# First-layer rows of blocks 3 to 7: turned by TensorE, or by VectorE on the way through DRAM

## The chip, the core and the metric

The kernel runs on one core of a Trainium2 chip. The time is device microseconds (us) of one execution; the profile is of a separate execution of the same program. Engines are named as the profile names them: PE is TensorE (PEld its weight loads), DVE is VectorE, ACT is ScalarE, POOL is GpSimd, and SP is the engine whose queue issues the transfers.

## What is computed

Two layers, each an attention with a learned feature map followed by a dense part, with the same weights in both layers. There are 2048 rows of 640 values in fp32, 32 heads of 20, and 1536 hidden values.

```
x = x + A(layernorm(x)) ; x = x + B(layernorm(x))        # twice

A: q, k, v = x @ wqkv
   phi(y) = [softmax(y w_phi), softmax(-y w_phi)]        # per head, 20 -> 40
   kv = phi(k)^T v ;  z = sum of phi(k)
   o  = phi(q) kv / (phi(q) z + 1e-6) ;  o @ wo
B: mish(x @ w1 + b1) @ w2
layernorm: (x - mean) / sqrt(var + 1e-5), over the 640 values of a row
```

## The kernel before, in words

**Tiles.** The rows are worked on in 8 blocks (numbered 0 to 7) of 256, each of two tiles (t = 0, 1) of 128 rows. A product is made of three: each operand is split into a high part and the remainder (low part), and high x high, high x low and low x high are added in PSUM. So a projection of one tile to 640 columns is 30 matmuls of 128x320 (L344): 5 pieces of the inner dimension, 2 halves of the columns, 3 products.

**Turned rows.** The matmuls need the rows with the 640 values along the partitions. The class `Transposed` (from L265) holds a block's rows in that form, as five pieces of 128 values by 256 rows. Its method `step` makes two pieces at a time (one in the third step): ScalarE's copy makes the high part `xth`, VectorE's subtraction (L286) makes the low part `xtl`. What a step copies comes from one of two places. If the object was given rows, TensorE transposes them (L280, ten transposes of 128x128 per block, against an identity) into a PSUM tile `one`. If it was given columns, these are tiles in SBUF that hold the rows turned already.

**How rows get turned without TensorE.** `spill_turned` (L311) has VectorE transpose each tile in 32x32 pieces, in place (L315), and stores it with four transfers (L317) to a DRAM tensor, in such an order that the tensor holds the block turned. Its pieces are 32 values, 128 bytes. `load_turned` (L319) reads the block back with three transfers (L325) into the tiles it is given. The dense part uses the pair for its own rows (`n1_d`) and for the second layer's first half (`n2_d`).

**The first half of a layer**, `attend_first` (L387), goes through the blocks. A block has six jobs, one per iteration n of the inner loop: keys of both tiles (k0, k1), values (v0, v1), queries (q0, q1), in an order that differs in blocks 0, 1 and 7. A job is a generator. Its first piece is the projection and ScalarE's copy out of PSUM (the `mm` tile; there are two). In the following iterations `advance` takes every pending job one piece further: maximum, minimum and differences (VectorE, for queries partly GpSimd), exponential (ScalarE), sums and reciprocals (VectorE) and the product (GpSimd, L379). A key job ends with 22 matmuls for the key-value product (L416). A query job ends with VectorE's transpose in place (L425) and four stores to `e_d` (L429). The next query job of the same tile t uses the same SBUF buffer `r`, so its copy out of PSUM waits for these stores.

**The next block's rows** are prepared beside the jobs. In the first layer `fetch_normed` (L390) fetches block b + 1 at n = 0 and takes its row statistics (`norm_stats` L246 on VectorE: L250 and L252; `norm_scale` L255 on GpSimd and VectorE). At n = 2 `normed` (L299) has ScalarE normalize both tiles into tiles `xn`, and at n = 3, 4, 5 the three steps with TensorE's transposes follow. In the second layer `fetch_normed` only calls `load_turned` on `n2_d`, into three `xn` tiles, and the steps at n = 3, 4, 5 read these.

**Buffers.** Two for x (`xt`), four for `xn`, two PSUM tiles `mm`, four PSUM tiles `one`.

**What sets the order.** The whole program stands in one block that a planner schedules: it simulates the engines with modelled times and puts on each engine the earliest instruction of the program that can run then, so that a later one may go ahead of one that waits. Transfers and statistics so come much earlier than written: block 7's x, written at block 6, is fetched in block 4. On the chip each engine then runs its list strictly in order. Two things are fixed by hand: all calls of `act` are chained (L110), so ScalarE does them in the order written, and the second half of the layer, `attend_second` (L553), has a written order for PE and SP.

Of the kernel before, what the change touches and what calls it, by code (L numbers as in the profile page):

```python
# [8 lines left out]
F32 = mybir.dt.float32  # L9
# [9 lines left out]
D = 640  # L19
# [5 lines left out]
BT = 2  # L25
BLK = BT * P
NB = S // BLK
# [15 lines left out]
def kernel(  # L43
# [56 lines left out]

    e_d = [dram.tile([EW, BLK], F32, name=f"e_d{b}") for b in range(NB)]

    n1_d = [dram.tile([D, BLK], F32, name=f"n1_d{b}") for b in range(NB)]
    n2_d = [dram.tile([D, BLK], F32, name=f"n2_d{b}") for b in range(NB)]
    x1_d = dram.tile([S, D], F32, name="x1_d")
# [149 lines left out]
    def norm_scale(b, mvs):  # L255

        ve = work.tile([P, BT], F32, tag="ve", name="ve", bufs=2)
        for t in range(BT):
            nc.gpsimd.tensor_scalar(ve[:, t:t + 1], mvs[t][:, 1:2], LN_EPS, 1.0, op0=ALU.add, op1=ALU.mult)
        nc.gpsimd.tensor_tensor(stats[:, b, 0], ve, neg_half, op=ALU.pow)  # L260
        for t in range(BT):
            nc.vector.scalar_tensor_tensor(stats[:, b, 1, t:t + 1], mvs[t][:, 0:1], -1.0,
                                           stats[:, b, 0, t:t + 1], op0=ALU.mult, op1=ALU.mult)
# [35 lines left out]
    def normed(b, xt):  # L299

        xn = [row_tile() for _ in range(BT)]
        for t in range(BT):
            act(xn[t], xt[:, t, :], AF.Identity,
                                 bias=stats[:, b, 1, t:t + 1], scale=stats[:, b, 0, t:t + 1])
        return Transposed(xn)

    def normalize(b, dst, src):
        for t in range(BT):
            act(dst[t], src[t], AF.Identity, bias=stats[:, b, 1, t:t + 1], scale=stats[:, b, 0, t:t + 1])
# [9 lines left out]
    def load_turned(src, tiles):  # L319

        cols = []
        for c, make in zip(range(0, KD, 2), tiles):
            n = min(2, KD - c)
            cols.append(make()[:, :n * BLK].rearrange("p (k s) -> p k s", k=n))
            nc.sync.dma_start(cols[-1], src[c * P:(c + n) * P].rearrange("(k p) s -> p k s", p=P))  # L325
        return Transposed(cols=cols)
# [55 lines left out]
    def fetch(x_src, b, xt=None):  # L382
        xt = x_tile() if xt is None else xt
        nc.sync.dma_start(xt, row_block(x_src, b))
        return xt

    def attend_first(layer, x_src, first):  # L387


        def fetch_normed(b):  # L390
            if layer:
                return load_turned(n2_d[b], [row_tile] * 3)
            xt = fetch(x_src, b)
            norm_scale(b, [norm_stats(t, xt) for t in range(BT)])
            return xt

        pending = []

        def advance():
            for g in pending[::-1]:  # L400
                try:
                    next(g)
                except StopIteration:
                    pending.remove(g)

        def keys(xts, i, v):
            e = big_tile()
            yield from features(project(xts, i % BT, kv_ws, 0), e, False)
            yield
            if i % BT == 0 and BT < i < NT - BT:  # L410
                yield
            for g in range(G):
                p, n = divmod(g, 2)
                w, m = (120, 64) if g < 10 else (80, 42)
                acc, c = (kva, 120 * p) if p < 4 else (kvz, 120 * (p - 4))
                nc.tensor.matmul(acc[64 * n:64 * n + m, c:c + w], v[:, GW * g:GW * g + m],  # L416
                                 e[:, 120 * g:120 * g + w],
                                 start=(i == 0 and p in (0, 4)), stop=(i == NT - 1),
                                 skip_group_check=True)

        def queries(xts, i, ps=None):
            e = query_tile(i)
            yield from features(project(xts, i % BT, q_ws, 0) if ps is None else ps, e, True)

            nc.vector.transpose(e, e)  # L425
            b, t = divmod(i, BT)
            dst = e_d[b].rearrange("(j f) (t q s) -> t q f j s", f=32, t=BT, s=32)
            for q in range(4):
                nc.sync.dma_start(dst[t, q], e[32 * q:32 * q + 32].rearrange("f (j s) -> f j s", s=32))  # L429
                if b == NB - 1:  # L430
                    yield

        def values(xts, i, v):
            vv = v.rearrange("p (h d) -> p h d", d=DH + 1)
            act(vv[:, :, DH], ident[:, :H], AF.Copy, scale=0.0, bias=1.0)
            if i < BT:
                pv = project(xts, i, kv_ws, D, [one_tile(), one_tile()])
                for c in range(2):
                    act(vv[:, c * H // 2:(c + 1) * H // 2, :DH],
                        pv[c][:, :HC].rearrange("p (h d) -> p h d", d=DH), AF.Copy)  # L440
            else:
                pv = project(xts, i % BT, kv_ws, D)
                act(vv[:, :, :DH].rearrange("p (c h) d -> p c h d", c=2),
                    both(pv).rearrange("p c (h d) -> p c h d", d=DH), AF.Copy)
            yield

        if first is None:
            with tc.manual_schedule(engines={mybir.EngineType.SP}):
                bd = big_tile()[:120, :720].rearrange("p (t c) -> p t c", t=6)
                nc.sync.dma_start(bd[:, :3], phi_bd[:, :3])  # L450
                raw = load_raw(0, range(3))
                xt = fetch_normed(0)
                nc.sync.dma_start(bd[:, 3:], phi_bd[:, 3:])
                raw += load_raw(0, range(3, 6))
                nxt = normed(0, xt).all()
                q_ws = [r2_pair(k) for k in range(KD)]
                fold_phi(q_ws, bd, raw)
                kv_ws = load_v_weights()
                raw = load_raw(1)
            nc.sync.dma_start(mask, head_mask)  # L460
        else:
            nxt, kv_ws = first
            q_ws = load_q_weights()
        for b in range(NB):
            xts = nxt
            order = ("k0", "k1", "v0", "v1", "q0", "q1")
            if b == 0:
                order = ("v0", "q0", "v1", "k0", "q1", "k1")
            elif b == 1:
                order = ("k0", "q0", "k1", "v0", "q1", "v1")  # L470
            elif b == NB - 1:
                order = ("k0", "k1", "v0", "v1", "q0")
            vs = [v_tile() for _ in range(BT)]
            for n, (kind, t) in enumerate(order):
                t = int(t)
                i = b * BT + t
                if b == 0 and n == 1:
                    if layer:
                        load_k_weights(kv_ws)
                if b == 0 and n == 3:  # L480
                    if layer == 0:
                        fold_phi(kv_ws, bd, raw)
                    kva, kvz = one_tile(), one_tile()
                if b == NB - 1 and n == 3:
                    loaded = {0: load(0)}
                if b + 1 < NB:
                    if n == 0:
                        xt = fetch_normed(b + 1)
                    elif n == 2:
                        nxt = xt if layer else normed(b + 1, xt)  # L490
                    elif n > 2:
                        nxt.step()
                g = {"k": lambda: keys(xts, i, vs[t]), "q": lambda: queries(xts, i),
                     "v": lambda: values(xts, i, vs[t])}[kind]()
                next(g)
                advance()
                pending.append(g)
            if b == 1:
                if layer == 0:
                    spill_qk_weights(kv_ws, q_ws)  # L500
                o_ws = load_o_weights()

        def rest():

            ps = [one_tile(), one_tile()]
            project_half(ps[0], xts, 1, q_ws, 0, 0)
            advance()
            advance()
            yield
            project_half(ps[1], xts, 1, q_ws, 0, 1, range(3))  # L510
            yield
            project_half(ps[1], xts, 1, q_ws, 0, 1, range(3, KD))
            pending.append(queries(xts, NT - 1, ps))
            next(pending[-1])
            while pending:
                yield
                advance()

        return kva, kvz, o_ws, loaded, rest()
# [379 lines left out]
```

## Time and profile before

| | |
|---|---|
| median of 3 runs | 1398.45 us (1397.73 to 1398.7) |
| profiled execution | 1396.09 us, of which the span of its instructions is 1394.3 us |
| granted TensorE clock | 0.999 of full speed |
| first layer, first half | from the start to about 271 us |
| second layer, first half | from about 743 to 948 us |
| idle time of ScalarE that ended with a transpose (L280) | 99.6 us, 21 times, over the whole program |

The profile's page gives each engine's busy time over the span. A timeline lists the instructions of a stretch by start, duration, engine, line, and tiles written and read; a note in brackets at the end is idle time of the engine just before, and what ended it. The chain of waits follows the work that ended last back from the end of the program. A matmul's duration there is the time that it is in flight, and the next one starts before it has ended; how far apart they start is what they cost.

### The profile page before, as it was taken

Reading aid. Unit: us, or ns where it says so; the run is one execution under the profiler, and the core shown is the slowest. Engines: PE = TensorE matmul, PEld = TensorE weight load, DVE = VectorE, ACT = ScalarE, POOL = GpSimd, SP = SyncE. Lnnn points to the kernel's source line nnn. Section 1 sums busy time; section 2 is a strip of 40 time slices with the busy share of each in tenths; the row PEclk is TensorE's granted clock in tenths of the full one; section 3 lists DMA queues with packets and bytes.
Section 4 is the critical chain, followed back from the end, with each engine's and each line's share of the span. In section 5 each row is a group of like instructions: output and inputs, shape, how many; then the busy total and the mean of one; then the engine's idle time right before and its main releaser. Section 6 shows DMA issues by size and latency. Waiting matters only on the chain. (4 is left out here: it accounts for less than half of the span.)

```text
span 1394.3 us, 28137 instructions
## 1 busy us (share of the span) xinstructions
PE 1380.7 (99%) x11528; PEld 1367.0 (98%) x11528; DVE 1075.5 (77%) x1820; ACT 583.3 (42%) x973; POOL 440.0 (32%) x334
## 2 busy tenths in 40 slices
PE   7999999999999999999999999999999999999998
PEld 7999999999999999999999999999999999999998
DVE  5797877796698877788769988888767876777775
ACT  4444433321355454545454333332235444444443
POOL 1353443343422221222234434343342211211112
PEclk9999999999999999999999999999999999999999
DMA  8533333689633432343474333357976212333200
GB/s 328 162 79 54 67 52 58 184 228 307 235 86 95 114 84 62 83 114 95 122 261 87 71 57 58 65 107 231 288 257 200 76 25 72 95 95 95 75 22 20
DMA packets 350035, 169.57 MB, mean 122 GB/s; under 512 B 286866, under 2 KB 323458, under 8 KB 349906
## 3 DMA queue, kind: packets, MB, share of 16 engines
q1 hardware_dynamic: 349906, 167.78, 44.2%
q8 instruction: 90, 1.47, 0.4%
q14 instruction: 39, 0.32, 0.1%
HBM read 104.82 MB, written 62.91 MB: 120 GB/s over the span
## 5 line engine op out<-in xcount | busy, mean ns | idle before, releaser
L737 PE MATMUL mm<-r2h,ol 128*128 128x320 f32 x1280 | 304.7, 309 | 0.0
L721 POOL TENSOR_TENSOR ol<-big,ol 128x512 fp32r<-128x512 f32 (+1 forms) x98 | 129.8, 1324 | 483.5 <-ACT ol L720 407.3
L695 PE MATMUL one<-xtl,r1h 128*128 128x256 f32 x960 | 268.2, 279 | 0.0
L695 PE MATMUL one<-xth,r1l 128*128 128x256 f32 x960 | 268.0, 279 | 0.0
L695 PE MATMUL one<-xth,r1h 128*128 128x256 f32 x960 | 265.9, 279 | 0.0
L737 PEld LDWEIGHTS mm<-r2h,ol 128*128 128x128 f32 x1280 | 219.1, 188 | 0.0
L737 PE MATMUL mm<-r2l,ol 128*128 128x320 f32 x640 | 197.3, 309 | 0.0
L344 PE MATMUL mm<-r1h,xth 128*128 128x320 f32 x600 | 187.3, 312 | 0.0
L344 PE MATMUL mm<-r1h,xtl 128*128 128x320 f32 x600 | 186.0, 310 | 0.7 <-DVE xtl L286 0.7
L344 PE MATMUL mm<-r1l,xth 128*128 128x320 f32 x600 | 186.0, 310 | 0.0
L695 PEld LDWEIGHTS one<-xtl,r1h 128*128 128x128 f32 x960 | 180.4, 188 | 0.0
L695 PEld LDWEIGHTS one<-xth,r1l 128*128 128x128 f32 x960 | 180.4, 188 | 0.0
L695 PEld LDWEIGHTS one<-xth,r1h 128*128 128x128 f32 x960 | 179.6, 188 | 0.0
L710 DVE TENSOR_SCALAR big<-big 128x512 f32<-128x512 f32 (+1 forms) x98 | 57.1, 583 | 109.9 <-ACT big L708 109.7
L379 POOL TENSOR_TENSOR r<-r,r 128x1280 f32<-128x1280 f32 x32 | 75.8, 2368 | 163.1 <-DVE r L378 157.3
L737 PEld LDWEIGHTS mm<-r2l,ol 128*128 128x128 f32 x640 | 120.2, 188 | 0.0
L712 ACT ACTIVATE big<-big,two 128x512 f32<-128x512 f32 (+1 forms) x98 | 70.1, 715 | 116.2 <-DVE big L711 116.1
L708 ACT ACTIVATE big<-one,b1s 128x256 f32<-128x256 f32 x192 | 80.8, 467 | 90.1 <-PE one L695 89.6
L720 ACT ACTIVATE ol<-big 128x512 fp32r<-128x512 f32 (+1 forms) x98 | 61.0, 622 | 136.0 <-DVE big L719 135.9
L344 PEld LDWEIGHTS mm<-r1h,xth 128*128 128x128 f32 x600 | 112.8, 188 | 1.3
L344 PEld LDWEIGHTS mm<-r1h,xtl 128*128 128x128 f32 x600 | 112.7, 188 | 1.3 <-DVE xtl L286 1.0
L344 PEld LDWEIGHTS mm<-r1l,xth 128*128 128x128 f32 x600 | 112.8, 188 | 0.1
(129 smaller groups left out, 3156.1 us busy)
## 6 DMA issues: line engine op xcount, KB each, us to landing
e_d<-r SPq DMA_DIRECT2D x128, 160.0 KB, 4.0
big<-e_d SPq DMA_DIRECT2D x32, 640.0 KB, 6.6
x_d<-xt SPq DMA_DIRECT2D x23, 640.0 KB, 3.9
xt<-x_d SPq DMA_DIRECT2D x22, 640.0 KB, 4.3
n_d<-xn SPq DMA_DIRECT2D x176, 80.0 KB, 2.1
xt<-in_x SPq DMA_DIRECT2D x16, 640.0 KB, 5.9
xn<-x_d SPq DMA_DIRECT2D x28, 320.0 KB, 4.2
v<-n_d SPq DMA_DIRECT2D x30, 256.0 KB, 3.3
```

Of the source, the lines that this page charges most:

```text
L344: nc.tensor.matmul(ps[:, :HC], a[:, sl], r, start=(k == 0 and n == 0), stop=(k == KD - 1 and n == 2))
L379: nc.gpsimd.tensor_tensor(eg, eg, r.unsqueeze(2).to_broadcast([P, 2 * H, DH]), op=ALU.mult)
L695: nc.tensor.matmul(ph[:, j, :], l, r, start=(n == 0), stop=(n == 3 * KD - 1))
L708: exps[0] = nc.scalar.activation(part(ta, 0)[:, j - js.start], ph[:, j, :], AF.Exp, bias=b1s[:, 2 * pr + j:2 * pr + j + 1]).ins
L710: nc.vector.tensor_scalar_min(e, e, E_CAP)
L712: nc.scalar.activation(r, n, AF.Ln, bias=two)
L720: nc.scalar.activation(ah[:, js], n, AF.Copy)
L721: nc.gpsimd.tensor_tensor(al[:, js], n, ah[:, js].bitcast(F32), op=ALU.subtract)
L737: nc.tensor.matmul(pys[t][:, c, :HC], l[:, j, sl], r, start=(f == 0 and n == 0), stop=(f == KF - 1 and n == 2))
```

## The change

In the first layer, blocks 3 to 7 take the way through DRAM that the second layer's blocks take. A DRAM tensor `n0_d` is added for each block. A generator `turn(b)` prepares such a block in four pieces: fetch x; statistics and scale; normalize in place, in the x tile; transpose by VectorE, in place, and store to `n0_d`. Block b's loop starts `turn(b + 3)` at n = 4 (the fetch), and the following block's loop runs its other pieces at n = 1, 2 and 3. One block later `fetch_normed` loads the turned rows at n = 0, and the steps at n = 3, 4 and 5 read them from SBUF. Blocks 1 and 2 stay as they were, block 0 too. x still has two buffers.

```diff
@@
+    n0_d = [dram.tile([D, BLK], F32, name=f"n0_d{b}") for b in range(NB)]
     n1_d = [dram.tile([D, BLK], F32, name=f"n1_d{b}") for b in range(NB)]
@@ attend_first
+        def turned(b):
+
+            return layer or b > 2
+
+        def turn(b):
+
+            xt = fetch(x_src, b)
+            yield
+            norm_scale(b, [norm_stats(t, xt) for t in range(BT)])
+            yield
+            rows = [xt[:, t, :] for t in range(BT)]
+            normalize(b, rows, rows)
+            yield
+            spill_turned(rows, n0_d[b])
+            yield
+
         def fetch_normed(b):
-            if layer:
-                return load_turned(n2_d[b], [row_tile] * 3)
+            if turned(b):
+                return load_turned((n2_d if layer else n0_d)[b], [row_tile] * 3)
@@ the loop over a block's jobs
                     elif n == 2:
-                        nxt = xt if layer else normed(b + 1, xt)
+                        nxt = xt if turned(b + 1) else normed(b + 1, xt)
                     elif n > 2:
                         nxt.step()
+                if not layer:
+                    if 0 < b < NB - 2 and n in (1, 2, 3):
+                        next(ahead)
+                    if n == 4 and b + 3 < NB:
+                        ahead = turn(b + 3)
+                        next(ahead)
```

## Prediction

> **What bounds the kernel now.** I read the page's totals first, then the chain of waits, then timelines and windows of the first layer's blocks (numbered from 0) beside the second layer's, which already load turned rows from DRAM.
>
> ```profile
> span 1394.3 us, 28137 instructions
> ...
> PE 1380.7 (99%) x11528; PEld 1367.0 (98%) x11528; DVE 1075.5 (77%) x1820; ACT 583.3 (42%) x973; POOL 440.0 (32%) x334
> ```
>
> TensorE works for 99% of the span, so an instruction taken from it shortens the span unless something else becomes late. The next rows, from the chain of waits in the second layer's first half, show a block without transposes, what ten transposes cost side by side (in the second half), and the one place where the chain left TensorE there.
>
> ```profile
> 772.18 0.98 DVE xtl L286
> ...
> 832.79 2.47 PE one L416 x43
> 835.26 26.60 PE mm L344 x180
> 861.86 2.47 PE one L416 x43
> ...
> 998.48 1.09 PE one L280 x10
> ```
>
> The key-value matmuls (L416) come once a block: from 832.79 to 861.86 is 29.07 us, which is 26.60 + 2.47, with no idle time. In the first layer the same mark is, in two TensorE timelines,
>
> ```profile
> 122.29 0.53 PE L416 MATMUL one<-big,v 128*64 128x120 f32 x6
> ...
> 242.99 1.25 PE L416 MATMUL one<-big,v 128*64 128x120 f32 x20
> ```
>
> Four blocks take 242.99 - 122.29 = 120.70 us, 30.175 each. The difference, 30.175 - 29.07 = **1.105 us a block**, is the ten transposes: the chain's row has ten in 1.09 us. The mean of one must not be used:
>
> ```profile
> L280 PE MATMUL one<-ident,xn 128*128 128x128 f32 x260 | 37.2, 279 | 0.0
> ```
>
> 279 ns is how long one is in flight, and they overlap: 1.09 / 10 = 109 ns is what one keeps from its successor. The Trainium skill (TensorE: Matmul & The Clock Gate, Part 4: PE-mode transpose) gives about 275 ns for one in a kernel; by that price 50 of them would give 13.8 us. The trace agrees with the duration and not with the price, and the spacing decides.
>
> **The change part by part.**
>
> *Removed:* the transposes of blocks 3 to 7, 5 x 10, so 5 x 1.105 = **5.5 us** off TensorE. Their evictions stay, but read SBUF.
>
> *Added to VectorE.* The windows are a crowded early stretch, a first-layer block without row statistics, and a second-layer block; the columns are us, PE, PEld, DVE, ACT, POOL, clock, DMA share, GB/s.
>
> ```profile
> 65.00:93.00 28.00, 28.00 (x231) 27.07 (x230) 28.00 (x34) 12.17 (x17) 17.83 (x11) 1.00 0.28 63
> 183.40:212.80 29.40, 29.40 (x230) 29.08 (x229) 22.66 (x27) 11.52 (x17) 11.98 (x6) 1.00 0.31 46
> 832.70:861.80 29.10, 29.10 (x227) 28.78 (x226) 24.82 (x28) 10.53 (x15) 12.16 (x6) 1.00 0.39 68
> ```
>
> ```profile
> L315 DVE STREAM_TRANSPOSE xn<-xn 128x640 f32<-128x640 f32 x44 | 36.3, 834 | 2.0 <-ACT xn L116 1.9
> ```
>
> Each turned block gets two transposes of this shape: 2 x 0.83 = 1.6 us with their overlap. Its three low-part subtractions (L286) read two SBUF tiles instead of PSUM and SBUF. First layer, then second:
>
> ```profile
> 167.91 1.66 DVE L250 BATCH_NORM_STATS2 bn<-xt 128x6 f32<-128x320 f32 x4
> 169.49 0.67 DVE L286 TENSOR_TENSOR xtl<-one,xth 128x512 fp32r<-128x512 f32 x1
> ...
> 173.41 0.68 DVE L286 TENSOR_TENSOR xtl<-one,xth 128x512 fp32r<-128x512 f32 x1
> ...
> 175.98 0.41 DVE L286 TENSOR_TENSOR xtl<-one,xth 128x256 fp32r<-128x256 f32 x1
> ...
> 840.64 1.54 DVE L368 TENSOR_REDUCE m<-big 128x32 f32<-128x640 f32 x2 [2.21 <-ACT big L116]
> ...
> 848.16 1.80 DVE L286 TENSOR_TENSOR xtl<-xn,xth 128x512 fp32r<-128x512 f32 x1
> ...
> 853.09 0.67 DVE L286 TENSOR_TENSOR xtl<-xn,xth 128x512 fp32r<-128x512 f32 x1
> ...
> 855.54 1.50 DVE L286 TENSOR_TENSOR xtl<-xn,xth 128x256 fp32r<-128x256 f32 x1
> 859.08 1.55 DVE L368 TENSOR_REDUCE m<-r 128x32 f32<-128x640 f32 x2 [2.04 <-ACT r L116]
> ```
>
> They take 1.80 + 0.67 + 1.50 = 3.97 us against 1.76: 2.2 more a block. With 24.82 us of the second layer's block, 1.6 for the transposes and about 2.0 for statistics where a block has them (the 1.66 above and their small followers), VectorE is busy 26.4 to 28.4 of 29.07 us. It fits, barely.
>
> *What that delays.* VectorE runs without a gap from 840.64 to 857.04, the end of the third subtraction (the rows left out between show no idle time). Its reader is the next block's first projection:
>
> ```profile
> 857.30 0.31 PE L344 MATMUL mm<-r1h,xth 128*128 128x320 f32 x1
> ```
>
> The third pair of the rows is read by the 13th of its matmuls, at 857.30 + 12 x 0.148 (26.60 / 180) = 859.07. **The slack is 2.0 us.** The transposes' 1.6 fit into it; 1.6 + 2.0 with statistics in the same stretch do not. I take the transposes at nothing in blocks 2 to 5. Their bounds are 0 (the gaps of 2.21 and 2.04 us above swallow them) and 1.6 a block, 8.0 in all.
>
> *Block 1* is worse. In 65 to 93 us VectorE has no idle time at all, and its last subtraction for block 2 ends at 89.56, 0.7 us ahead of the matmul that reads it:
>
> ```profile
> 89.20 0.36 DVE L286 TENSOR_TENSOR xtl<-one,xth 128x256 fp32r<-128x256 f32 x1
> ```
>
> ```profile
> 90.30 0.41 PE L344 MATMUL mm<-r1h,xtl 128*128 128x320 f32 x1
> ```
>
> Block 3's transposes fall in here. Block 4's statistics, which stand here now, move behind block 3's spill, but block 5's take their place, because block 2's x buffer comes free at the same point. So 1.6 - 0.7 = **0.9 us of new stall**, once. Below it could be 0 (a statistic moves out), above it 1.6 + 2.0 - 0.7 = 2.9.
>
> *Statistics* keep their count. Blocks 6 and 7 fetch into buffers that blocks 4 and 5 hold until spilled, so their rows arrive late in blocks 2 and 3, behind the third subtraction: 0, and 1.6 each (3.6 - 2.0) if the planner puts them ahead of it.
>
> *ScalarE:*
>
> ```profile
> 70.24 1.72 ACT L116 ACTIVATE xn<-xt,stats 128x640 f32<-128x640 f32 x2
> 71.87 0.68 ACT L116 ACTIVATE big<-mm 128x640 f32<-128x640 f32 x1
> ```
>
> ```profile
> 76.73 0.39 PE L344 MATMUL mm<-r2h,xth 128*128 128x320 f32 x1
> ```
>
> Each normalization stands one or two blocks earlier, the count is the same. Block 1 gets two of them, so the eviction queued behind (ScalarE keeps its written order) moves from 71.87 to 73.6; its PSUM buffer is next written by the projection at 76.73, so this costs nothing. At 42% load ScalarE hides the rest.
>
> *Queue SP* issues all transfers in order.
>
> ```profile
> 163.16 0.35 SPq L384 DMA_DIRECT2D xt<-in_x  x1
> 163.61 12.86 SPq L429 DMA_DIRECT2D e_d<-r  x8
> ...
> 563.65 5.30 SPq L317 DMA_DIRECT2D n_d<-xn  x8
> ...
> 851.82 3.24 SPq L429 DMA_DIRECT2D e_d<-r  x4
> 855.16 2.28 SPq L325 DMA_DIRECT2D xn<-n_d  x2
> ```
>
> ```profile
> e_d<-r SPq DMA_DIRECT2D x128, 160.0 KB, 4.0
> ...
> n_d<-xn SPq DMA_DIRECT2D x176, 80.0 KB, 2.1
> ```
>
> A turned block adds eight spills (5.3 us of SP, landing 2.1 us after issue) and three loads (1.1 us each by the last row); the fetches remain. Two waits are new. A fetch into a spilled buffer waits for its spills; a load waits for its block's spills. Behind both stand the query stores (e_d), and for these waits an eviction:
>
> ```profile
> 858.34 0.71 ACT L116 ACTIVATE r<-mm 128x640 f32<-128x640 f32 x1 [4.18 <-DMA e_d<-r]
> ```
>
> It ends at 859.05; its PSUM buffer is needed by the second key projection, which follows the key-value matmuls at 861.86 + 2.47 = 864.33. That leaves 5.2 us. Transposes (1.6) and a landing behind the spills' packets (about 2.1, one landing) stay inside, so I count 0; all eight spills ahead (5.3) would not.
>
> **The sum** is made against the profiled execution, 1396.09 us (its span is 1394.3): - 5.5 + 0.9 = 1391.5. The median of the runs shown, 1398.45, is 2.36 above the profiled one; with that added, **1393.9 us**.
>
> **The rivals.**
>
> *No new stall (chance 0.13).* Statistics leave block 1: 1398.45 - 5.5 = 1392.9. For it: the second layer's blocks run at exactly 29.07. Against it: no slack in block 1, and 772.18 above, where a second-layer block did wait for a subtraction.
>
> *Third subtraction late, even (0.18).* The planner orders VectorE by modelled times. If it puts statistics and transposes ahead of the third subtraction in blocks 2 and 3, where both occur, the stalls are 0.9 + 2 x 1.6 = 4.1 us, the gain 1.4, the time 1397.
>
> *VectorE becomes the bound (0.15).* Mechanism: a subtraction with two SBUF inputs that starts while GpSimd works waits for it.
>
> ```profile
> 847.04 2.37 POOL L379 TENSOR_TENSOR r<-r,r 128x1280 f32<-128x1280 f32 x1 [6.11 <-DVE r L378]
> ```
>
> The 1.80 us one starts inside this instruction and ends 0.55 after it. Each further hit costs 1.13 us (1.80 - 0.67), and more VectorE work lets more of them overlap. With 1.6 + 2.0 + 1.13 ahead of the third subtraction the stall is 4.7 - 2.0 = 2.7 a block, 13.5 in five, less 5.5: + 8, **1406**. It decides from 3.1 us of added work there (2.0 slack + 1.1 saved). Against it: only blocks 2 and 3 may get statistics. The Trainium skill (SBUF — State Buffer, SBUF: two separate sides) has this rule: one of the two holds a shared port for its whole instruction and the other blocks. By that rule the change moves 15 subtractions into the contended form; the rows agree with it.
>
> *SP becomes late (0.09).* With all spills ahead, query stores come 1.6 + 5.3 = 6.9 us later, 1.7 past the 5.2 of slack: 8.5 in five blocks, + 3.0, 1401.4. Against it: SP is free between the stores of a block.
>
> *It doesn't do what it says:* with two x buffers, block 4 cannot be fetched before block 3 is spilled, so "three ahead" holds only for some. Even now the fetch at 163.16 is block 7's, issued in block 4. That changes no term.
>
> **How the numbers follow.** Forecast 0.45, no stall 0.13, even 0.18, VectorE bound 0.15, SP late 0.09. About 0.2% (2.8 us) is what a measurement here can tell from no change: faster is under 1395.65, which the first two give, 0.58; within 0.18; slower 0.15 + 0.09 = 0.24. The range runs from 1392.4 (no stall) to 1402 (SP late) and leaves out the VectorE bound, 0.15. The forecast's own range is 1392.9 to 1395.6.
>
> **What would show it.** First-layer periods of the key-value matmuls near 29.1 us from block 3 on; 50 fewer transposes; a wait of TensorE for L286 of about 1 us near 90 us; L286 with 1.5 to 1.8 us beside GpSimd; query evictions later, but before 5 us. Wrong if TensorE waits for L286 or for a PSUM buffer in each of blocks 2 to 6.

## The result, and the profile after

The changed kernel takes 1412.33 us (median of 4, 1409.29 to 1414.21) against 1398.3 for the kernel before: the ratio is 1.0099, with a 95% interval of 1.008 to 1.0117. It is **slower by 14 us**; the forecast was 1393.9, 4.4 us faster, and the range ended at 1402. The profiled execution is the fastest of the four (1409.29 us, mean granted clock 0.999); the other three took 1412.13 to 1414.21 us at 0.996 or 0.997, so some 3 us of lost clock, an estimate from these figures (0.002 of 1410), are in the median and not in the profile below.

In the rows of the changed kernel the line numbers are one higher than before up to line 385 (L281 transposes, L287 low-part subtraction, L318 spill, L326 load), and 17 higher from the jobs on (L433 key-value matmuls, L442 and L446 the queries' transpose and stores). From its page, the span and the engines' totals:

```profile
span 1407.5 us, 28144 instructions
...
PE 1379.5 (98%) x11478; PEld 1363.3 (97%) x11478; DVE 1095.3 (78%) x1830; ACT 584.0 (41%) x973; POOL 442.3 (31%) x334
```

Fifty matmul instructions are gone (11528 - 11478), and yet the span grew by 13.2 us (1407.5 - 1394.3). VectorE works 19.8 us more (1095.3 - 1075.5). TensorE's timeline has the mark of the prediction, the key-value matmuls, in each block:

```profile
159.22 2.54 PE L433 MATMUL one<-big,v 128*64 128x120 f32 x44 [0.74 <-POOL big L380]
...
198.95 2.54 PE L433 MATMUL one<-big,v 128*64 128x120 f32 x44
...
226.41 2.54 PE L433 MATMUL one<-big,v 128*64 128x120 f32 x44
...
255.48 2.54 PE L433 MATMUL one<-big,v 128*64 128x120 f32 x44
```

From 226.41 to 255.48 is 29.07 us, to the hundredth the period that was forecast without transposes. But from 159.22 to 198.95 is 39.73. The mark shifts a little within a block, so this has to be read together with the 27.46 that follow: the two are 9 us longer than twice 29.07. What TensorE waited for between 40 and 270 us is listed by the view of waits (engine and line that waited, engine and line that it waited for, us in total, times, the longest). The kernel before has no row there; the changed one has these:

```profile
PE mm L345 <- ACT r L117: 5.8, 4, 2.7
PE mm L345 <- DVE xtl L287: 4.4, 4, 2.2
PE mm L345 <- ACT xth L117: 1.7, 1, 1.7
PE one L433 <- POOL big L380: 0.7, 1, 0.7
PE mm L345 <- DVE r1l L244: 0.3, 1, 0.3
```

That is 12.9 us. The first row is the late copy of a query out of PSUM (it holds up a PSUM buffer), the second the low part of the next block's rows. Behind the first layer's first half the two kernels run nearly alike: the changed one is 12.4 us late at 290 us and 13.2 at the end. As it has 5.5 us less to do, about 18 us were lost by then: 12.9 in these waits and 1.7 to a halved clock in block 4 (see the last section); about 3 are not placed.

**Where the waits come from: block 2.** SyncE's queue, VectorE and TensorE in the changed kernel, one after the other:

```profile
110.23 5.87 SPq L318 DMA_DIRECT2D n_d<-xt  x8
118.30 0.90 SPq L326 DMA_DIRECT2D xn<-n_d  x2
119.24 0.47 SPq L385 DMA_DIRECT2D xt<-in_x  x1
119.75 6.45 SPq L446 DMA_DIRECT2D e_d<-r  x4
```

```profile
125.30 0.89 DVE L251 BATCH_NORM_STATS2 bn<-xt 128x6 f32<-128x320 f32 x2 [1.85 <-DMA xt<-in_x]
126.11 0.41 DVE L287 TENSOR_TENSOR xtl<-xn,xth 128x256 fp32r<-128x256 f32 x1
```

```profile
126.57 0.41 PE L345 MATMUL mm<-r1h,xtl 128*128 128x320 f32 x1 [0.77 <-DVE xtl L287]
```

Read it backwards. TensorE waits for the third subtraction. This stands in VectorE's list behind the statistics of a later block, and they wait 1.85 us for the x of block 6, which ScalarE normalizes only at 170 us. The fetch of x was issued at 119.24, because it goes into the buffer that had just been spilled and stands behind loads, and these wait until the spills have landed: the last spill is issued at 110.23 + 5.87 = 116.10, the loads at 118.30. The query stores stand behind all of it.

**Block 4**, where most of the time is lost, shows what such waits become, on SyncE's queue, ScalarE, VectorE and TensorE:

```profile
145.22 6.45 SPq L318 DMA_DIRECT2D n_d<-xt  x8
153.64 0.90 SPq L326 DMA_DIRECT2D xn<-n_d  x2
154.58 3.77 SPq L446 DMA_DIRECT2D e_d<-r  x4
```

```profile
161.44 0.70 ACT L117 ACTIVATE r<-mm 128x640 f32<-128x640 f32 x1 [11.08 <-DMA e_d<-r]
...
186.37 0.70 ACT L117 ACTIVATE r<-mm 128x640 f32<-128x640 f32 x1 [3.30 <-DMA e_d<-r]
```

```profile
162.17 1.55 DVE L369 TENSOR_REDUCE m<-r 128x32 f32<-128x640 f32 x2 [5.22 <-ACT r L117]
165.18 1.67 DVE L251 BATCH_NORM_STATS2 bn<-xt 128x6 f32<-128x320 f32 x4 [1.46 <-DMA xt<-in_x]
...
168.21 0.81 DVE L372 TENSOR_TENSOR r<-m,r 128x640 f32<-128x640 f32 x1
...
178.25 1.49 DVE L442 STREAM_TRANSPOSE r<-r 128x1280 f32<-128x1280 f32 x1
...
190.59 0.98 DVE L287 TENSOR_TENSOR xtl<-xn,xth 128x256 fp32r<-128x256 f32 x1
```

```profile
187.12 0.42 PE L345 MATMUL mm<-r1h,xth 128*128 128x320 f32 x1 [2.66 <-ACT r L117]
191.63 0.41 PE L345 MATMUL mm<-r1h,xtl 128*128 128x320 f32 x1 [2.18 <-DVE xtl L287]
197.15 0.41 PE L345 MATMUL mm<-r1h,xth 128*128 128x320 f32 x1 [1.54 <-ACT r L117]
```

A query's transpose ends at 152.08, but its stores are issued only at 154.58, 2.5 us later, behind loads that wait until the spills have landed. The copy of the next query into that buffer waits for the stores until 161.44, and VectorE 5.22 us for this copy. This query job's second piece (168.21) then stands behind the statistics that wait for x. Its transpose comes at 178.25, its stores follow, and the copy of the next query into the same buffer waits for them until 186.37; the third subtraction, queued on VectorE behind all of this, comes at 190.59. TensorE pays three times, 6.4 us together.

**Blocks 0 and 1.** Here are two windows of the same stretch, before and after (us, then PE, PEld, DVE, ACT, POOL, granted clock, DMA share, GB/s):

```profile
60.00:105.00 45.00, 45.00 (x360) 43.76 (x359) 44.97 (x55) 19.68 (x27) 24.00 (x14) 1.00 0.41 83
```

```profile
60.00:105.00 45.00, 40.91 (x314) 39.31 (x313) 42.92 (x57) 18.30 (x26) 24.01 (x17) 1.00 0.52 104
```

VectorE was busy for 44.97 of 45.00 us before the change already. In the groups by line for VectorE, 58 to 103 us before and 58 to 112 after (the same jobs, nearly), what was put on top can be counted:

```profile
L369 DVE TENSOR_TENSOR big<-big,m 128x640 f32<-128x640 f32 x5 | 6.2, 1234 | 0.0
...
L250 DVE BATCH_NORM_STATS2 bn<-xt 128x6 f32<-128x320 f32 x4 | 1.7, 474 | 0.0
```

```profile
L370 DVE TENSOR_TENSOR big<-big,m 128x640 f32<-128x640 f32 x5 | 8.5, 1700 | 0.0
...
L251 DVE BATCH_NORM_STATS2 bn<-xt 128x6 f32<-128x320 f32 x8 | 3.3, 475 | 0.0
L316 DVE STREAM_TRANSPOSE xt<-xt 128x640 f32<-128x640 f32 x4 | 3.1, 799 | 0.0
```

Two blocks' statistics stand there instead of one (1.6 us more, and 1.1 for the small instructions that follow them), and the transposes of two blocks (3.1). The difference of the keys above takes 2.3 us more with the same count, but two other rows of differences go from 5.4 to 3.6 and from 3.8 to 4.6, so all differences take 1.3 more. Together that is 7 us in a stretch without room. TensorE started 314 matmuls in the 45 us instead of 360 and stood idle for 4.1 (45.00 - 40.91): 1.13 for a query's copy at 74 us, 1.66 for a high part at 94, 1.28 for the subtraction at 99. Some of the expectations below speak of 7 to 8.2 us in blocks 0 and 1; these were read from the mark, which shifts, and the idle time is the better figure.

### The profile page after: what moved, and what is told of

The parts are those of the page before. It is cut to its first block, busy times and chain, and to the rows that moved or that the text cites. A ratio compares the mean times of both kernels' runs of the same rounds, so it can differ in the third digit from the quotient of the medians.

```text
span 1407.5 us, 28144 instructions
## 1 busy us (share of the span) xinstructions
PE 1379.5 (98%) x11478; PEld 1363.3 (97%) x11478; DVE 1095.3 (78%) x1830; ACT 584.0 (41%) x973; POOL 442.3 (31%) x334
```

## The experiments

Differences below are medians against the kernel before, run on the same chip; the changed kernel stands at + 14.0. A version with four runs has an interval of about 2 us to each side, so less than 3 us between two of them is not clear of noise. The theories were named as follows. **S:** the order on SyncE's queue makes the query stores late. **V:** VectorE's 1.6 us of turning per block do. **E:** blocks 0 and 1 get a new order when blocks 3 and 4 are turned by VectorE. **X,** added after the first four runs: statistics stand in VectorE's list at a place where x has not come yet.

**Stores first, all blocks.** The spills and the loads of a block are held behind its second query's stores.

```diff
+                with behind():        # issue after the query stores
+                    next(ahead)       # the spills
...
+                            with behind():
+                                xt = fetch_normed(b + 1)   # the loads
```

> The changed kernel, but from block 1 on the spills of a turned block, and the loads of one, are issued behind the query stores of tile 1 that are written ahead of or beside them (an order between transfers only). Theory S (on the queue SP the eight spills, and the loads that wait for their landing, stand ahead of these stores, so a query eviction and then TensorE come late): blocks 2 to 6 lose their stalls, about 9 us of block 4's 10.7 us over its 29.07 us and a little elsewhere, so about 1402 us. Theory V (VectorE has too much to do and comes late by itself): the evictions stay late, within 3 us of the changed kernel's 1412. Theory E (blocks 0 and 1 are late since the planner ordered them anew, 8.2 us by the marks of the key-value matmuls): those 8.2 us stay here in either case.

Measured: 1409.56 us, + 11.3 (ratio 1.0078, 1.0061 to 1.0094). S gave back 2.8 us, which is not clear of noise, and not the 10 that S was to give. VectorE's timeline tells why:

```profile
172.71 1.67 DVE L251 BATCH_NORM_STATS2 bn<-xt 128x6 f32<-128x320 f32 x4 [3.89 <-DMA xt<-in_x]
```

With spills and loads later, the fetch behind them is later too, and VectorE waits 3.89 us for x instead of 1.46. One wait was exchanged for another; this row made theory X.

**No turning by VectorE.**

```diff
-            nc.vector.transpose(rows[t], rows[t])
```

This is done for `n0_d` only; the spills store the rows as they are.

> The changed kernel without VectorE's transposes of blocks 3 to 7 in the first layer: their rows are spilled and loaded as they are, so the values are not the reference's, all transfers stay. Takes 10 x 0.83 us from VectorE. Theory V: evictions and third subtractions come 1.6 us a block earlier and more where delays add up, about 5 to 8 us off, 1404 to 1407. Theory S: spills start earlier but stand in the same places, under 3 us off, 1410 or so. Theory E: 8.2 us in blocks 0 and 1 stay.

Measured: 1400.32, + 2.1 (1.0014, 1.0005 to 1.0023). From 159.67 us on the periods are 29.06 and 29.07 us, and TensorE waits nowhere after 127 us; what is lost lies ahead of that, in blocks 0 to 2 (waits of 1.85 and 1.81 us, with a halved clock behind each). So 11.9 us came off, where V allowed 5 to 8: without VectorE's transposes the later blocks have room, and the early ones lose all the same.

**From block 5 on; and the same with the stores first.**

```diff
-            return layer or b > 2
+            return layer or b > 4
...
-                    if 0 < b < NB - 2 and n in (1, 2, 3):
+                    if 2 < b < NB - 2 and n in (1, 2, 3):
-                    if n == 4 and b + 3 < NB:
+                    if n == 4 and 5 <= b + 3 < NB:
```

> The changed kernel with only blocks 5, 6 and 7 turned by VectorE, so that no turned block is worked on before block 3. TensorE is spared 3 x 1.1 = 3.3 us. Theory E: blocks 0 and 1 take their old times, 8.2 us less than in the changed kernel; if blocks 3 to 5 then lose nothing, 1395; if a block loses 9 us as block 4 did, 1404. Theory S alone: the queue's order in blocks 3 to 5 is the same as before, so a stall of some 9 us, 1404. Theory V: 2 of 5 blocks less, about 1405.

> Blocks 5, 6 and 7 turned, and spills and loads behind the query stores (both of the edits beside it). Theory S with theory E: no stall is left, 1398.3 - 3.3 = 1395. Theory V: VectorE still has 1.6 us more in each of three blocks and statistics in some, 1398 to 1405.

Measured: 1404.4, + 6.2 (1.0042, 1.0027 to 1.0057), and with the stores first 1397.91, - 0.3 (1.0, 0.9991 to 1.0009). In both the first periods are those of before (14.48 and 24.6 us by the key-value mark): E holds. TensorE's waits, without and with the new order of the queue:

```profile
PE mm L345 <- ACT r L117: 6.3, 3, 2.2
```

```profile
PE mm L345 <- ACT r L117: 0.4, 1, 0.4
```

The query copies' 6.3 us go down to 0.4, and the time falls by 6.5: here S is all of it.

**x in a tile of the keys' pool,** alone and with the stores first. The turned blocks' x no longer needs the buffer of a block that is still being spilled.

```diff
-            xt = fetch(x_src, b)
+            xt = fetch(x_src, b, big_tile().rearrange("p (t d) -> p t d", t=BT))
```

> The changed kernel, but x of the turned blocks is fetched into a free tile of the keys' pool instead of one of the two x buffers, so that a fetch no longer waits for an earlier block's spill. Theory X (VectorE stands in line for x that comes late, and the queries behind it come late): no wait of VectorE for x of 1 us or more in blocks 3 to 5, block 4's period falls from 39.7 to about 31 us, 1402 to 1406 us. Theory S (stores behind loads on SP) and theory V (the 1.6 us of turning by itself): little changes, 1409 to 1414. Theory E (new order in blocks 0 and 1) keeps its 7 us in both.

> Both remedies at once on all five blocks: x in a tile of the keys' pool, and spills and loads behind the query stores of their block. X and S together: only the early blocks' 7 us are left against the 5.5 gained, 1398 to 1401 us, periods of about 29 us from block 3 on. X alone: as the run with x in a key tile, within 1.5 us. V: 1406 or more, with waits of TensorE for query copies in blocks 3 to 5.

Measured: 1407.39, + 8.9 (1.0062, 1.0047 to 1.0077); with both remedies 1405.14, + 6.7 (1.0043, 1.0028 to 1.0058). VectorE no longer waits for x in blocks 2 to 5 of either, and that gave 5.1 us; the order of the queue gave 2.2 more, which is not clear of noise. X holds, but it is smaller than expected (1402 to 1406 us), and both together did not reach 1398 to 1401. With both remedies TensorE waits in these places (a fourth row, 0.7 us in all, is left out):

```profile
PE mm L345 <- ACT r L117: 2.4, 2, 1.4
PE one L437 <- POOL big L380: 2.1, 1, 2.1
PE mm L345 <- ACT xth L117: 0.9, 1, 0.9
```

The second and the third row fall at 93 and 95 us, in block 1, and behind them comes something that no theory had named. The windows of that stretch (us, TensorE's busy time, granted clock, DMA share, GB/s) show the clock at half; the last section shows when it falls:

```profile
90.00:95.00 5.00, 2.39 (x28) 0.94 0.29 40
95.00:100.00 5.00, 4.56 (x16) 0.50 0.02 3
100.00:105.00 5.00, 5.00 (x32) 0.88 0.77 115
```

Adding up (1 - clock) x 5 us gives 3.4 us lost, more than the 3.0 of the two waits.

**Block 3 left to TensorE,** with both remedies on blocks 4 to 7 (`b > 3`, and the loop's bounds one higher); and **from block 5** with both remedies.

> Both remedies, and block 3 stays with TensorE: only blocks 4 to 7 are turned. E holds block 3's turning to blame for the early blocks: the first two periods are those of before (14.5 and 25.8 us), and 1394 to 1396 us comes out (4 x 1.1 saved, up to 1 lost). If block 4's fetch and statistics disturb the early blocks as well, 1398 to 1402. V: 1402 or more.

> Both remedies, blocks 5 to 7 turned by VectorE, block 3 and 4 by TensorE. If each block from 4 on is worth its 1.1 us less a stall of about 0.5: 1397.3 to 1398.0, a little above the run from block 4 (1397.1). If x in the keys' pool frees what the run from block 5 with the stores first (1397.9) still lost: 1395.5 to 1396.5.

Measured from block 4: 1397.08, - 1.4 (0.9987, 0.9978 to 0.9996), **the only version with all of the work that beats the kernel before by its interval,** and by little. From block 5: 1397.8, - 0.8 (0.9992, 0.9983 to 1.0001). Turning block 3 by VectorE costs 8.1 us net (6.7 + 1.4). VectorE waits 2.87 us for x here too, at 106 us, and TensorE doesn't wait before 153 us: a late x costs nothing where nothing urgent stands behind it. TensorE's waits from block 4 on:

```profile
PE mm L345 <- ACT r L117: 2.6, 2, 1.6
```

**The kernel before with VectorE's transposes alone.** They turn the x tile in place after it has been normalized, and nobody reads it.

```diff
+                        if not layer and b + 1 > 2:
+                            for r in range(BT):
+                                nc.vector.transpose(xt[:, r, :], xt[:, r, :])
```

> The kernel before, with nothing of the change but VectorE's two transposes of 128x640 per block for blocks 3 to 7, in place in the x tile after it has been normalized; nobody reads them, TensorE still turns the rows, and there are no spills, loads or early fetches. V (the 1.6 us by themselves make the queries late): stalls of TensorE in each block from 2 on, 1403 us or more. X, S and E: VectorE has the room, 1398 to 1400.

Measured: 1400.28, + 1.8 (1.0015, 1.0005 to 1.0024), a little above what X, S and E allowed and far below V's 1403. Five blocks' turning costs 1.8 us if it is all that is added. V as a cause by itself has fallen. But the same transposes cost 11.9 us in the changed kernel, where the rest stands beside them.

**What of block 3 costs so much.** Five runs with both remedies on blocks 3 to 7 leave out parts of block 3's preparation, the last one (only loaded) the fetch and the spills too. The comments are added here; where only statistics go, block 3 is normalized with block 2's.

```diff
-            spill_turned(rows, n0_d[b])
+            spill_turned(rows, n0_d[b], b > 3)      # no transposes
...
-            norm_scale(b, [norm_stats(t, xt) for t in range(BT)])
+            if b > 3:                               # no statistics
+                norm_scale(b, [norm_stats(t, xt) for t in range(BT)])
...
-            normalize(b, rows, rows)
+            if b > 3:                               # no normalization
+                normalize(b, rows, rows)
```

> The run with both remedies on blocks 3 to 7 (1405.1 us), with VectorE's two transposes left out for block 3 alone, so that the values of block 3 are wrong; its statistics, spills and loads stay. Against the run that leaves block 3 to TensorE (1397.1) 8.1 us are to be explained. If the transposes in the full stretch of VectorE (block 1) are the cause: 1398 to 1400. If statistics are: 1403 to 1405. If spills and loads are: 1404 to 1405.

> As the run with both remedies on blocks 3 to 7, but without row statistics for block 3, which is normalized with block 2's, so that its values are wrong; the transposes stay. If it is any VectorE work in block 1 that counts, the 2.5 us of statistics that go give 2.5 to 4 back: 1401 to 1403. If the transposes alone: 1404 to 1406.

> As the run with both remedies on blocks 3 to 7, with neither statistics nor VectorE transposes for block 3 (its values are wrong); its fetch, normalization by ScalarE, spills and loads stay. If VectorE's added work in block 1 is what block 3 costs: the run from block 4 less one block's TensorE transposes, 1396 to 1398. If the spills, loads or ScalarE's earlier normalization cost it: 1402 or more.

> As the run with neither statistics nor VectorE transposes for block 3 (1400.6 us), and without ScalarE's normalization of block 3 as well (its values are wrong); fetch, spills and loads of block 3 stay. If the normalization, which stands in block 1 ahead of the copies there, costs the 3.5 us that were left against the run from block 4 (1397.1): 1396 to 1398. If spills and loads or the planner's order do: 1399.5 to 1401.

> Block 3 is only loaded, as if it lay turned in DRAM (it reads other rows of x, so its values are wrong): no fetch, statistics, normalization, transposes or spills for it; blocks 4 to 7 as with both remedies. The run from block 4 less one block's TensorE transposes: 1395.5 to 1396.5. If it stays above 1399, it is the planner's order alone.

| block 3 without | us | difference | ratio, 95% | 85 to 135 us: idle + half clock |
|---|---|---|---|---|
| nothing left out | 1405.14 | + 6.7 | 1.0028 to 1.0058 | 3.1 + 3.4 |
| transposes | 1401.68 | + 3.1 | 1.0009 to 1.0028 | 3.0 + 1.7 |
| statistics | 1400.25 | + 1.6 | 1.0004 to 1.0023 | 2.0 + 0 |
| both | 1400.58 | + 2.0 | 1.0004 to 1.0023 | 1.4 + 0 |
| both and the normalization | 1399.18 | + 0.2 | 0.9993 to 1.0011 | 0.9 + 0 |
| all but the loads | 1399.56 | + 0.6 | 0.9997 to 1.0015 | 0.8 + 0 |
| left to TensorE (from block 4) | 1397.08 | - 1.4 | 0.9978 to 0.9996 | 0 + 0 |

The last column is from one profile each: the time in which TensorE stood idle between 85 and 135 us, and what it lost there to the halved clock.

The transposes (1.6 us of work) give back 3.6 us when they go, the statistics (1.7 us of L251 and their small followers) 5.1, and both together no more than the statistics. So the prices do not add up, and by the medians each part alone takes off more than its length. The last column says why, for the profiled executions: what block 3 costs is waits in that stretch and, in the first two versions, the halved clock behind them. It falls in nearly the same order as the times. None of the first three came out where an expectation had put it: no single part is the cause. The normalization gives perhaps 1.8 more (the intervals overlap), the spills nothing that shows. The version that only loads block 3 is above 1399 (its interval reaches down to 1398.5), which by its expectation leaves the planner's order; it is 2.0 us above the one that leaves block 3 to TensorE. TensorE's waits there:

```profile
PE mm L346 <- ACT r L117: 3.1, 2, 2.0
PE mm L346 <- DVE xtl L287: 1.4, 2, 0.8
```

The second row is what is new against the run from block 4: 1.4 us of waiting for low parts. That they are late because block 4's preparation stands elsewhere in VectorE's list was argued and not shown; this remainder stays open.

**Blocks 3 to 7 only loaded,** as if they lay in DRAM turned: no fetch, statistics, normalization, turning or spills.

> All of blocks 3 to 7 are only loaded, as if they lay turned in DRAM (values wrong): the removed term by itself. 50 transposes at 1.105 us a block: 5.5 below before, 1392.5 to 1393.5, with first-layer periods of 29.07 us. At the 275 ns of one in flight it would be 13.8 us: 1384.7. More than 5.5 if VectorE's statistics and ScalarE's normalization, which are left out too, had cost something before.

Measured: 1393.82, - 5.1 (0.9963, 0.995 to 0.9975). TensorE's marks:

```profile
123.30 2.54 PE L447 MATMUL one<-big,v 128*64 128x120 f32 x44
...
239.58 2.54 PE L447 MATMUL one<-big,v 128*64 128x120 f32 x44
```

Four blocks in 116.28 us, 29.07 each. The removed term was right, and sparing VectorE and ScalarE the statistics and the normalization as well brought nothing beyond it.

## Why the prediction was wrong, step by step

*TensorE bounds, and 50 transposes are worth 5.5 us:* right. The run that only loads measures 5.1 (3.5 to 7.0 by its interval), and blocks without a stall have the forecast period. 5.1 us over 50 transposes is 103 ns each, and the row with the spacing (109) decides. The Trainium skill (TensorE: Matmul & The Clock Gate, Part 4: PE-mode transpose) states about 275 ns for one in a kernel; by that price the estimate would have been 13.8 us.

*"I take the transposes at nothing in blocks 2 to 5":* right in size where they stand alone (1.8 us for all five), wrong in this kernel, where they are not alone: taking them out of the changed kernel gives back 11.9 us, more than the bound of 8.0.

*"Their rows arrive late in blocks 2 and 3, behind the third subtraction: 0":* **this step failed first.** The planner put the statistics into VectorE's list ahead of the third subtraction and of the queries, by a modelled landing of x, and VectorE, which takes its list in order, waited for the real one: 1.85 us at 125 us and 1.46 at 165 us. The bound that I gave, 1.6 each, was the instructions' own time and not the wait for x. I had noted that the fetch must wait for a spilled buffer, and had written that this changes no term. Fetching x into another tile gave back 5.1 us.

*SyncE's queue, counted 0 for 5.2 us of slack:* **failed.** The slack was measured in the second layer, where the stores stand ahead of the loads. Here loads and a fetch stand ahead of the stores and wait for a landing, while the queries themselves came later on VectorE: the slack was used up by the other term. The order alone gave back 2.2 to 2.8 us with blocks 3 to 7, not clear of noise, and 6.5 from block 5 on, which is.

*"0.9 us of new stall, once" in block 1:* **the largest miss.** The mechanism was right (VectorE has no idle time there, and the forecast wait for the subtraction came, 1.28 us at 99 us), the size was not: in the changed kernel TensorE stands idle for 4.1 us there, and with both remedies turning block 3 costs 8.1 us net, 9.1 with its share of the gain (5.1 / 5 = 1.0). I added 1.6 us for the transposes and let the statistics cancel out; in fact two blocks' statistics stood there, and the lateness reached a query's copy and a high part as well. The sum also had no term for the clock: with both remedies the profile has 3.1 us of waits in block 1 and 3.4 lost to the halved clock behind them. My upper bound, 2.9, was a sum of instructions alone.

*ScalarE 0:* nearly. The earlier normalization costs perhaps 1.8 in block 1, within noise; that it does so through the copies queued behind it was not shown.

*The rivals.* "VectorE becomes the bound" came nearest in time (1406), by another mechanism: it expected a loss in every block from contended subtractions, but blocks 5 and 6 ran at 27.46 and 29.07 us. "SP late" had the right place; of its 8.5 us in five blocks the order of the queue gave back 2.2 to 2.8. "Third subtraction late" named the step that failed first, at 1.6 us a block, but with x in time; its waits for the subtraction came, 4.4 us in four places. None of them had two waits that feed each other, and none the clock.

From + 14.0 down, in measured steps: x in another tile - 5.1, the stores first - 2.2, block 3 left to TensorE - 8.1, which gives - 1.4. Another order of the steps splits it otherwise, as the 11.9 us without VectorE's transposes show. Against the pure gain for four blocks (4/5 of 5.1 = 4.1) 2.7 us are still lost, about the 2.6 us for which TensorE waits for query copies in the version from block 4.

## What to carry to other kernels

An engine that is busy for all of a stretch has no price list there: what is added can cost more than its length (1.6 us of transposes gave back 3.6), since what stands behind it pays as well and the clock can fall behind the waits, so the stretch with the least slack is to be costed first, with every instruction that the new order puts into it. A prefetch into a buffer that must first be drained through DRAM is only as early as the drain; where an in-order engine has it in its list ahead of urgent work, its lateness is the urgent work's lateness. Slack that was read in one loop must not be spent twice, once for the queue and once for the engine that feeds it.

## What the runs showed of the hardware

**A short stall can halve the clock after it.** In the run without VectorE's transposes TensorE waits 1.85 us at 75 us, and 1.4 us after it has resumed its matmuls spread out:

```profile
75.25 0.41 PE L346 MATMUL mm<-r1h,xth 128*128 128x320 f32 x1 [1.85 <-ACT r L117]
...
76.24 0.31 PE L346 MATMUL mm<-r1h,xth 128*128 128x320 f32 x1
76.39 0.31 PE L346 MATMUL mm<-r1l,xth 128*128 128x320 f32 x1
...
77.99 0.47 PE L346 MATMUL mm<-r1h,xtl 128*128 128x320 f32 x1
78.25 0.47 PE L346 MATMUL mm<-r1h,xth 128*128 128x320 f32 x1
```

The windows of that stretch, with the granted clock in the third column from the end:

```profile
76.00:78.00 2.00, 2.00 (x12) 2.00 (x11) 2.00 (x3) 2.00 (x4) 1.27 (x1) 0.68 0.00 0
78.00:80.00 2.00, 2.00 (x9) 2.00 (x9) 2.00 (x3) 2.00 (x3) 0.00 (x0) 0.50 0.49 84
```

Starts are 0.15 us apart, then 0.26, and the clock is down to 0.50. The half clock lasts from 76.70 to 80.11 us, so half of 3.41, 1.7 us, is lost, nearly as much as the stall. It is not the length of a stall alone that decides: with x in the keys' pool a stall of 3.34 us passed at full clock.

```profile
159.12 0.41 PE L345 MATMUL mm<-r1h,xth 128*128 128x320 f32 x1 [3.34 <-ACT r L117]
```

What decides shows when a trace is cut into stretches. In each trace the clock changes only at times that lie whole multiples of 3.413 us apart (without VectorE's transposes at 76.70, 80.11, 127.90 and 131.31 us; 127.90 - 76.70 is 15 x 3.413). Cut at these times, TensorE's busy time in a stretch and the clock in the next one are:

| version | stretch, us | busy of 3.41 | idle share | clock in the next |
|---|---|---|---|---|
| without VectorE's transposes | 73.29 to 76.70 | 1.56 | 0.54 | 0.50 |
| the same | 124.49 to 127.90 | 1.60 | 0.53 | 0.50 |
| changed kernel | 185.61 to 189.03 | 1.91 | 0.44 | 1.00 |
| the same | 189.03 to 192.44 | 1.23 | 0.64 | 0.50 |
| x in the keys' pool | 153.96 to 157.37 | 1.82 | 0.47 | 1.00 |
| the same | 157.37 to 160.78 | 1.66 | 0.51 | 1.00 |
| the same | 188.09 to 191.50 | 0.97 | 0.72 | 0.50 |
| block 3 without normalization | 183.32 to 186.73 | 1.66 | 0.51 | 0.50 |

The stall of 3.34 us lay across two stretches and filled about half of each; the one of 1.85 us lay in one. In the traces of all versions, from 30 us on, the clock fell after every stretch that was idle for 0.53 or more and after none up to 0.48; at 0.51 it fell once and once it didn't. The ends of matmuls are modelled, so the shares are not exact. A fall lasted one stretch, and two in the version with both remedies (94.41 to 101.23 us). Where the stretches begin differs between executions, so the same waits can cost a fall in one and not in another; how far that explains the spread of the times was not shown.

The Trainium skill (TensorE: Matmul & The Clock Gate, Part 1: The HAM clock gate) puts the fall to half behind an idle window of about 3.4 us, in a window that runs freely. The two levels (1.00 and 0.50) and the length of the window (3.41 us) agree with the traces; that the window is idle throughout was not needed here, a little over half of it was enough.
